# Down projection with the last 64 rows of its contraction as pairs of 64-row tiles, and a new order of all steps

## The chip, the cores and the metric

The kernel runs on one core of one Trainium2 chip. The metric is the device time of one execution in microseconds. The kernel before takes 234.98 us in the median of three runs (234.88 to 235.36). All inputs are bf16 in HBM, and so is the output.

## What is computed

Two independent branches read the same layer-normalised input and are added to it. Branch A is a gated long convolution (a four-tap shift convolution of k, times v, a convolution of length 2048 by FFT, times the normalised input). Branch B is a gated feed-forward layer.

```python
S, D, F = 2048, 640, 1728
xn = layernorm(A_q)
# branch A
k_shift = sum(k_pad[t:t + S] * shift_k[:, 3 - t] for t in range(4))
kv = k_shift * v
y = irfft(rfft(kv padded to 2 S) * rfft(ssm_k padded to 2 S))[:S] + kv * ssm_D
A = xn * y
# branch B
h = sigmoid(xn @ w_gate) * (xn @ w_up)        # 2048 x 1728
Bo = h @ w_down                               # 2048 x 640
out = A_q + A + Bo
```

## The kernel before

The 2048 tokens lie on 128 partitions with 16 blocks of 128 tokens each. x, the normalised xn, all weights and the output stay in SBUF; the result is added into x in place and stored from there.

**Branch B** goes in four stages t = 0 to 3 of 512 tokens (four blocks bb). In a stage, the 1728 hidden columns are 13 tiles of 128 and one of 64. For each of the 13, gate_mm and up_mm make two products of five matmuls of 128x512 each (product, L291), gate_ev takes the sigmoid on ACT (L300), up_ev multiplies on DVE and writes hT[:, fc, :] (L306). The last 64 gate columns and the last 64 up columns share one product (both_mm, L312): its upper 64 partitions hold the up half, and both_mul (L321) writes the 64 hidden rows to partitions 64 to 127 of hT[:, 13, :]. Partitions 0 to 63 of that tile are cleared once (L126), and so are those of wd[:, 13, :] (L127).

The down projection sums 14 tiles, fc = 0 to 13, for each token block. The first 512 output columns are down_mm (L329), 14 matmuls of 128x512 in two parts of seven, into one PSUM bank pd; down_ev (L334) adds the bank to x on DVE. The remaining 128 columns are rest_mm (L340), 14 matmuls of 128x128 for each block, and rest_ev (L345).

**Branch A** goes in five chunks c of 128 channels. Taps and products are on DVE (kv_op, L373 to L382), ssm_k is turned in place (h_turn, L359), and the transform has two stages of matmuls each way: st1_mm (L398, L400), through DRAM (wr1, rd2), st2_mm (L432, 32 matmuls of 32x32 tiles), a complex product on DVE (prod, L445 and L447), inv1_mm (L461, 32 matmuls of 32x32 tiles), through DRAM again (wr2, L477 and L481; rdb, L491), and inv2_mm (L500, eight matmuls of 128x128). inv2_q (L505) multiplies by xn, inv2_x (L510) adds to x. PSUM results of st1, st2 and inv1 are copied out by ACT (act_copy, L254) or by DVE (dve_copy, L257).

**PSUM.** Two pools share the eight banks: psC has two tiles of two banks (st1, st2, inv1), psG four tiles of one bank (gate, up, both, pd, pr, psb of inv2).

**The order** is written out by hand. Each kind of step fills a chain under a letter (from L565 on), and the string ORDER (L683) says which chain gives the next step: g is PE's work of branch B, s its ACT part, u its DVE part, a/b/c/d the matmuls of branch A, A/B/C their copies on ACT, I/F/J the same on DVE, p prod, q inv2_q and inv2_x, k kv_op, w/r/W/R the transfers through DRAM, m and n the loads, o the stores. TURNS (L694) permutes the loads and the stores. Each engine executes its own instructions in this order, and waits on semaphores for the others. Nearly all DMAs are issued from SP's queue; the last store goes through ACT's (L348).

In a stage the steps of the down projection come as (bb, part) = (0,0), (1,0), (0,1), (1,1), (2,0), (2,1), with down_ev after each second part, then (3,0), (3,1) and the rest. In stage 3 the rest of blocks 0 to 2 comes ahead of block 3.

Of the kernel before, what the change touches and what calls it, by code (L numbers as in the profile page):

```python
# [10 lines left out]
BF16 = mybir.dt.bfloat16  # L11
# [6 lines left out]
DM = 640  # L18
FF = 1728
P = 128  # L20
NB = S // P
NC = DM // P
NFC = 14
# [42 lines left out]
def kernel(  # L66
# [14 lines left out]
    nc = tc.nc  # L81
# [15 lines left out]
    res = ctx.enter_context(tc.tile_pool(name="res", bufs=1))  # L97
# [22 lines left out]
    w = res.tile([P, NC, 2 * FF], BF16, name="w")  # L120
    wd = res.tile([P, NFC, DM], BF16, name="wd")
    hT = res.tile([P, NFC, 512], BF16, name="hT")
    kxs = [res.tile([P, NB + 3, P], BF16, name="kx%d" % i) for i in range(2)]
    for kx in kxs:
        nc.gpsimd.memset(kx[0:1, 0:3, :], 0.0)
    nc.gpsimd.memset(hT[0:64, 13, :], 0.0)  # L126
    nc.gpsimd.memset(wd[0:64, 13, :], 0.0)  # L127
    nc.vector.memset(hT[:, 0, :], 0.0)
    warm = res.tile([P, 4], F32, name="warm")
    nc.scalar.activation(warm[:, :], mhalf[:, :], ACT.Sigmoid)  # L130
# [60 lines left out]
    def load_wd(eng, lo, hi):  # L191
        h = min(hi, 13)
        eng.dma_start(wd[:, lo:h, :], B_w_down[lo * P:h * P, :].rearrange("(c p) e -> p c e", p=P))
        if hi == NFC:
            eng.dma_start(wd[64:P, 13, :], B_w_down[13 * P:FF, :])


    lns = [dict() for _ in range(4)]
# [121 lines left out]
    def both_mul(t):  # L320
        nc.vector.tensor_tensor(hT[64:P, 13, :], sig[13][64:P, :], pgs[2, 13][64:P, :], ALU.mult)  # L321

    pds = {}

    def down_mm(t, bb, part):
        if part == 0:
            pds[bb] = psG.tile([P, 4 * P], F32, name="pd", tag="g")
        for fc in range(7 * part, 7 * part + 7):
            nc.tensor.matmul(pds[bb][:, :], lhsT=hT[:, fc, bb * P:(bb + 1) * P], rhs=wd[:, fc, 0:4 * P],  # L329
                             start=(fc == 0), stop=(fc == NFC - 1))  # L330

    def down_ev(t, bb):
        b = 4 * t + bb
# [233 lines left out]
    def step(k, fn, *args):  # L567
        chains[k].append((fn, args))

    for t in range(4):  # L570
        for fc in range(0 if t else 2, 13):
            step("g", gate_mm, t, fc)
            step("s", gate_ev, t, fc)
            step("g", up_mm, t, fc)
            step("u", up_ev, t, fc)
        step("g", both_mm, t)
        step("s", both_ev, t)
        step("u", both_mul, t)
        for bb, part in ((0, 0), (1, 0), (0, 1), (1, 1), (2, 0), (2, 1)):
            step("g", down_mm, t, bb, part)  # L580
            if part:
                step("u", down_ev, t, bb)
        last = [(0, 3), (3, 4)] if t == 3 else [(0, 4)]
        for b0, b1 in last:
            if b1 == 4:
                step("g", down_mm, t, 3, 0)
                step("g", down_mm, t, 3, 1)
                step("u", down_ev, t, 3)
            for bb in range(b0, b1):
                step("g", rest_mm, t, bb, b0)  # L590
            step("u", rest_ev, t, b0, b1)
# [10 lines left out]
    for k in ((load_w, sync, 512, 768, 0),  # L602
              (load_w, sync, 512, 768, 1),
              (load_taps, 0),
              (sync.dma_start, SMt[:], SMd.ap()),
              (load_w, sync, 768, 1024, 0),
              (load_w, sync, 768, 1024, 1),
              (load_w, sync, 1024, 1280, 0),
              (load_w, sync, 1024, 1280, 1),
              (load_wd, sync, 0, 7),  # L610
              *ks(0),
              (load_w, sync, 1280, FF, 0),
              (load_w, sync, 1280, FF, 1),
              *hs(0),
              *vs(0),
              (load_wd, sync, 7, NFC),
              (sync.dma_start, S1t[:], S1d.ap()),
              (sync.dma_start, FWt[:], FWd.ap()),
              *hs(1),
              (load_x, sync, 1),  # L620
              *ks(1),
              *vs(1)):
        step("m", *k)
# [54 lines left out]
    for b in (0, 4, 8, 12):  # L678
# [2 lines left out]
    step("o", store, NB - 1, NB, 4 * P, DM)  # L681

    ORDER = """  # L683
    mmmmmggsmgggsuuggsgmLgLumssZLLPmguggumggmsgmkmkkuslgsTkmkukuggsummgsmmHHmmggugDkksumlggsgllugkkkkkkk
    kHHaamAnggAtkaaImueeggkuuwAagaeeAAkkLggkgmuDgamwLgsAaAwkkkkmgLgsKKaAgakukkkkkgusuggAsTkugagtwaLkkgsI
    AuuggkkkakhHHgwnsauKKsgVAAPlgsauklTwIkLkkrgaggruwVAVsDlbgklBuggBsawuagAAgbgkkssgkkKkFuuatkBhaIgkgAwm
    paakLsprswkgupukKKKHAAwggLpaaAkugAgceuggCCbkkkHDkgkkLgBFkkeuuaapggAeAVpTgeurbFPBpgstgrbkuBggwBkaaskk
    gguIgAsgkksuKVhHrkwawAWaAkggDaAparApukgnkpkssgcCVJuuggbFwBWggssubBBkwppgskgaaIuuggrAcgpJgrpsuCbsFRWk
    BgsugupbBprgsBllgugscCdlrpdkukkkwegeqqClHbBBRggbBgWrFqaeIagAdaaquqqupdpgAAppwaaAuggrAqqucCeJRwgggbpw
    WBFpgugbrrdqpqgsdRgBBpcuggJqCWbgsusFBgsubggBppdBdpqqppcrsCCrguugsbFgguBsRbpggrrBpBdcqqqsWdqCggpCuqpq  # L690
    bFBRpruggsbWpBBuqsggcpJCdqusgupbdWBBggsqppgsugRcCJuqqggRdqqsWgdRugdqqqdquRogggqogguuqooooddqqqqogddo
    qqgggoqoquuuoooo
    """
    TURNS = {"m": [6, 0, 1, 4, 21, 5, 13, 2, 7, 15, 9, 10, 12, 14, 8, 17, 18, 11, 16, 20, 22, 23, 19, 25, 24, 26, 3],  # L694
        "o": [5, 0, 6, 3, 1, 7, 4, 2, 8, 10, 9, 11, 12, 13]}
    left = {k: iter([v[i] for i in TURNS.get(k, range(len(v)))]) for k, v in chains.items()}
    for k in "".join(ORDER.split()):
        fn, args = next(left[{"F": "B", "J": "C", "I": "A", "Y": "E"}.get(k, k)])
# [32 lines left out]
```

## Time and profile before

| | us |
|---|---|
| median of the runs | 234.98 |
| the profiled execution | 235.94 |
| its span, first to last instruction | 234.2 |
| PE busy (matmuls) | 227.0 |
| DVE busy | 204.1 |
| ACT busy | 131.5 |
| POOL busy | 12.7 |
| matmuls of gate and up, L291: 250 each | 62.2 each |
| matmuls of down, L329 (213 of 224 recorded) | 50.4 |
| matmuls of the rest, L340 | 13.8 |
| granted TensorE clock | 1.00 |

The span is the time from the first to the last instruction of one profiled execution; the execution's own time has a little more around it. A row of the timeline gives the start in us from the span's start, the busy time, the engine, the line, the operation, out<-in by tile names, the shape and the count. Matmuls overlap: the row of one says 379 ns for 128x512, though the next one starts earlier, so pitches are read from starts.

### The profile page before, as it was taken

The numbers are of one execution on the slowest core, as the hardware profiler recorded it, in microseconds if no ns is written. First come the engines' busy times: TensorE is split into PE (matmuls) and PEld (weight loads), VectorE is DVE, ScalarE is ACT, GpSimd is POOL, SyncE is SP. The second block draws the span as 40 slices with busy tenths as digits, with TensorE's granted clock in tenths as the row PEclk, the third lists the DMA queues.
The fourth block names the chain that finished last, engine by engine and source line by source line (L and its number), as shares of the span: only waits on it lengthen the run. The fifth ranks groups of instructions, "written<-read, shape, count | busy, mean of one in ns | idle before, by whom it ended". The sixth has DMA issues, their size and how long they took to land.

```text
span 234.2 us, 5584 instructions
## 1 busy us (share of the span) xinstructions
PE 227.0 (97%) x2270; PEld 112.8 (48%) x2281; DVE 204.1 (87%) x323; ACT 131.5 (56%) x191; POOL 12.7 (5%) x27
## 2 busy tenths in 40 slices
PE   7799999999999999999999999999999999999993
PEld 2664444447444444446444444445563545445582
DVE  5532789999969999999999999999999999999574
ACT  2347832438985877866647666855555776652000
POOL 5201200000020000012001000000000000000000
PEclk9999999999999999999999999999999999999999
DMA  6999999799789987978879998999989769784775
GB/s 176 278 305 235 246 344 203 208 243 304 198 270 293 317 213 211 249 164 243 212 261 266 309 272 214 271 227 258 321 200 247 213 180 255 182 217 145 216 266 148
DMA packets 98143, 56.07 MB, mean 239 GB/s; under 512 B 56326, under 2 KB 92358, under 8 KB 97990
## 3 DMA queue, kind: packets, MB, share of 16 engines
q1 hardware_dynamic: 97542, 55.35, 88.2%
q10 hardware_dynamic: 576, 0.36, 0.5%
q8 instruction: 18, 0.29, 0.5%
q14 instruction: 7, 0.06, 0.1%
HBM read 35.39 MB, written 18.35 MB: 229 GB/s over the span
## 4 chain that ended last, share of the span: by engine, by line
PE 79%; DVE 12%; DMA 4%; issue 2%; SPq 1%; ACT 1%; DVEq 0%
PE pg L291 22%; PE pu L291 22%; PE pd L329 14%; PE psb L500 3%; PE pr L340 3%; PE ps L400 3%; PE ps L398 3%; DMA w<-in_B_w_up_dram 3%; PE ps L432 3%; PE psa L461 2%; DVE tmp L377 2%; PE pg L312 1%; DVE acc L379 1%; DVE yx L505 1%; DMA SMt<-tabSM 1%
## 5 line engine op out<-in xcount | busy, mean ns | idle before, releaser
L291 PEld LDWEIGHTS <-w 128*128 128x128 bf16 x500 | 47.1, 98 | 57.4 <-issue 4.0
L291 PE MATMUL pu<-xnT,w 128*128 128x512 bf16 x250 | 62.2, 379 | 0.0
L291 PE MATMUL pg<-xnT,w 128*128 128x512 bf16 x250 | 62.2, 379 | 0.0
L329 PE MATMUL pd<-wd,hT 128*128 128x512 bf16 x213 | 50.4, 379 | 0.7 <-issue 0.2
L306 DVE TENSOR_TENSOR hT<-sig,pu 128x512 bf16<-128x512 bf16 x52 | 34.6, 679 | 12.8 <-ACT sig L300 6.9
L254 ACT CAST t<-ps 128x1024 bf16<-128x1024 f32 x33 | 32.3, 1013 | 21.9 <-PE ps L400 21.9
L300 ACT ACTIVATE sig<-pg 128x512 bf16<-128x512 f32 x52 | 30.6, 598 | 23.7 <-PE pg L291 20.1
L254 ACT CAST xz<-ps 128x1024 bf16<-128x1024 f32 x30 | 29.5, 1015 | 14.3 <-PE ps L432 14.3
L329 PEld LDWEIGHTS <-hT 128*128 128x128 bf16 x224 | 21.3, 98 | 25.1 <-issue 0.9
L447 DVE TENSOR_TENSOR xz<-xz 128x2048 bf16<-128x2048 bf16 x20 | 24.4, 1218 | 0.3
L377 DVE TENSOR_TENSOR tmp<-kx,sc 128x1024 bf16<-128x1024 bf16 x30 | 20.9, 698 | 0.4
L379 DVE TENSOR_TENSOR acc<-acc,tmp 128x1024 bf16<-128x1024 bf16 x30 | 20.6, 685 | 0.5
L505 DVE TENSOR_TENSOR yx<-psb,xn 128x512 bf16<-128x512 f32 x20 | 13.8, 688 | 2.6 <-PE psb L500 1.8
L400 PE MATMUL ps<-kvh,S1t 128*128 128x512 bf16 x40 | 15.5, 387 | 0.0
L254 ACT CAST ao<-psa 128x1024 bf16<-128x1024 f32 x11 | 10.8, 1014 | 8.3 <-PE psa L461 8.2
L398 PE MATMUL ps<-kvh,S1t 128*128 128x512 bf16 x40 | 15.1, 379 | 0.0
L445 DVE STREAM_SHUFFLE xz<-xz 128x512 f32<-128x512 f32 x20 | 14.5, 725 | 0.0
L340 PE MATMUL pr<-wd,hT 128*128 128x128 bf16 x224 | 13.8, 219 | 0.0
L340 PEld LDWEIGHTS <-hT 128*128 128x128 bf16 x224 | 13.0, 98 | 1.8 <-issue 0.6
L334 DVE TENSOR_TENSOR x<-pd,x 128x512 bf16<-128x512 f32 x16 | 10.7, 684 | 2.1 <-PE pd L329 2.0
L257 DVE CAST xz<-ps 128x1024 bf16<-128x1024 f32 x10 | 12.1, 1215 | 0.4 <-PE ps L432 0.4
L500 PEld LDWEIGHTS <-TBt 128*128 128x128 bf16 x160 | 9.7, 98 | 3.4 <-issue 1.5
(57 smaller groups left out, 183.9 us busy)
## 6 DMA issues: line engine op xcount, KB each, us to landing
d<-t SPq DMA_DIRECT2D x20, 512.0 KB, 5.1
t<-d SPq DMA_DIRECT2D x20, 512.0 KB, 5.5
bi<-d SPq DMA_DIRECT2D x8, 512.0 KB, 5.3
d<-ao SPq DMA_DIRECT2D x6, 512.0 KB, 5.7
kvh<-in_A_v_dram SPq DMA_DIRECT2D x10, 256.0 KB, 5.3
kx<-in_A_k_dram SPq DMA_DIRECT2D x10, 256.0 KB, 4.6
hn<-in_A_ssm_k_dram SPq DMA_DIRECT2D x20, 128.0 KB, 4.6
x<-in_A_q_dram SPq DMA_DIRECT2D x3, 640.0 KB, 5.1
```

The source lines that it names most:

```text
L254: nc.scalar.copy(out=out, in_=in_)
L291: nc.tensor.matmul(pg[:, :], lhsT=w[:, c, u * UP + fc * P:u * UP + (fc + 1) * P], rhs=xnT[:, :, c, :], start=(c == 0), stop=(c == NC - 1))
L300: nc.scalar.activation(sig[fc][:, :], pgs[0, fc][:, :], ACT.Sigmoid)
L306: nc.vector.tensor_tensor(hT[:, fc, :], sig[fc][:, :], pgs[1, fc][:, :], ALU.mult)
L329: nc.tensor.matmul(pds[bb][:, :], lhsT=hT[:, fc, bb * P:(bb + 1) * P], rhs=wd[:, fc, 0:4 * P], start=(fc == 0), stop=(fc == NFC - 1))
L340: nc.tensor.matmul(pds[t, b0][:, bb, :], lhsT=hT[:, fc, bb * P:(bb + 1) * P], rhs=wd[:, fc, 4 * P:DM], start=(fc == 0), stop=(fc == NFC - 1))
L377: nc.vector.tensor_tensor(d["tmp"][:, :, :], kx[:, lo + 3 - m:hi + 3 - m, :], sb(m), ALU.mult)
L379: nc.vector.tensor_tensor(d["acc"][:, :, :], d["acc"][:, :, :], d["tmp"][:, :, :], ALU.add)
L398: nc.tensor.matmul(ps[:, 0, :, :], lhsT=S1[:, h, :], rhs=cin[c]["kvh"][:, 0, 4 * n4:4 * n4 + 4, :], start=True, stop=True)
L400: nc.tensor.matmul(ps[:, 1, :, :], lhsT=S1[:, h, :], rhs=hp[:, 2 * n4:2 * n4 + 2, :, :], start=True, stop=True)
L447: nc.vector.tensor_tensor(z[:, 1:3, :, :], z[:, 0:1, :, :].to_broadcast((P, 2, 8, P)), z[:, 1:3, :, :], ALU.mult)
L500: nc.tensor.matmul(ps[:, i, :], lhsT=TB[:, h, 4 * m + i, :], rhs=bi[:, h, 4 * (m % 2) + i, :], start=(h == 0), stop=(h == 1))
```

## The change

A small tile hA of 64 partitions is added. After both_mul, a new step both_copy on ACT copies the 64 hidden rows of blocks 0 and 2 from partitions 64 to 127 of hT[:, 13, :] to partitions 0 to 63 of hA. down_mm leaves out fc 13: its second part has six matmuls in place of seven. A new step pair_mm adds what is left for all four blocks: blocks 0 and 2 from hA with a copy of the last 64 rows of w_down on partitions 0 to 63, blocks 1 and 3 from hT on partitions 64 to 127. Blocks 0 and 1 then have all their terms, and blocks 2 and 3 get their second part afterwards. So four accumulators are open at the same time. The 512 columns of w_down's last rows are loaded twice, and POOL clears only the 128 columns left for the rest, which is computed as before.

```diff
+    hA = res.tile([64, 2, P], BF16, name="hA")
...
-    nc.gpsimd.memset(wd[0:64, 13, :], 0.0)
+    nc.gpsimd.memset(wd[0:64, 13, 4 * P:DM], 0.0)
...
             eng.dma_start(wd[64:P, 13, :], B_w_down[13 * P:FF, :])
+            eng.dma_start(wd[0:64, 13, 0:4 * P], B_w_down[13 * P:FF, 0:4 * P])
...
+    def both_copy(t):
+        nc.scalar.copy(out=hA[:, :, :], in_=hT[64:P, 13, :].rearrange("p (b e t) -> p b e t", b=2, e=2)[:, :, 0, :])
...
-        for fc in range(7 * part, 7 * part + 7):
+        for fc in range(7 * part, 7 + 6 * part):
             nc.tensor.matmul(pds[bb][:, :], lhsT=hT[:, fc, bb * P:(bb + 1) * P], rhs=wd[:, fc, 0:4 * P],
-                             start=(fc == 0), stop=(fc == NFC - 1))
+                             start=(fc == 0), stop=(bb > 1 and fc == NFC - 2))
+
+    def pair_mm(t):
+        for bb in range(4):
+            lhsT = hT[64:P, 13, bb * P:(bb + 1) * P] if bb % 2 else hA[:, bb // 2, :]
+            rows = slice(64, P) if bb % 2 else slice(0, 64)
+            nc.tensor.matmul(pds[bb][:, :], lhsT=lhsT, rhs=wd[rows, 13, 0:4 * P], start=False, stop=(bb < 2))
...
         step("u", both_mul, t)
-        for bb, part in ((0, 0), (1, 0), (0, 1), (1, 1), (2, 0), (2, 1)):
+        step("s", both_copy, t)
+        for bb, part in ((0, 0), (1, 0), (0, 1), (1, 1), (2, 0), (3, 0)):
             step("g", down_mm, t, bb, part)
-            if part:
-                step("u", down_ev, t, bb)
+        step("g", pair_mm, t)
+        step("u", down_ev, t, 0)
+        step("u", down_ev, t, 1)
+        step("g", down_mm, t, 2, 1)
+        step("u", down_ev, t, 2)
         last = [(0, 3), (3, 4)] if t == 3 else [(0, 4)]
         for b0, b1 in last:
             if b1 == 4:
-                step("g", down_mm, t, 3, 0)
                 step("g", down_mm, t, 3, 1)
                 step("u", down_ev, t, 3)
```

ORDER is another string throughout: the same steps with the new ones among them, in another interleaving of the two branches, with three more st2 copies on ACT and three fewer on DVE, and one inv1 copy the other way. TURNS is new too: the loads of weights, k, v and the convolution kernel and the stores come in another sequence. In the last stage inv1_mm(9), the last of its kind, stands after the first part of block 0 of the down projection (before: ahead of both_mm), one store stands between wr2(9) and the reads rdb(4,0) and rdb(4,1), and the last steps are down_mm(3,3,1), inv2_mm(4,3), rest_mm of block 3, with down_ev, inv2_q, rest_ev and inv2_x behind them on DVE. The end of the string, before and after:

```diff
-    WBFpgugbrrdqpqgsdRgBBpcuggJqCWbgsusFBgsubggBppdBdpqqppcrsCCrguugsbFgguBsRbpggrrBpBdcqqqsWdqCggpCuqpq
-    bFBRpruggsbWpBBuqsggcpJCdqusgupbdWBBggsqppgsugRcCJuqqggRdqqsWgdRugdqqqdquRogggqogguuqooooddqqqqogddo
-    qqgggoqoquuuoooo
...
+    CggJswqbpBFupggsdqbBpguWqrrBpdqgscCJqugugbFBgppsuRgbBpggsuddqWqBrrscCJRgugbqqppBBWspggsrbrBBggupupdd
+    RqcJgsCpgsubFBprggsbBBuggpsqqudcCdgqJbquWpRRBBpggWgsgsppuugcCgJdqqqqgqddqgdqqWogqqsggguguRdRuqooodqqq
+    qoggudoogoqqodguoqouoqoo
```

More of the change, by code (lines that the diff above doesn't have):

```diff
@@ L683 @@
     ORDER = """
[L684 to L689, printed above, removed]
-    WBFpgugbrrdqpqgsdRgBBpcuggJqCWbgsusFBgsubggBppdBdpqqppcrsCCrguugsbFgguBsRbpggrrBpBdcqqqsWdqCggpCuqpq
-    bFBRpruggsbWpBBuqsggcpJCdqusgupbdWBBggsqppgsugRcCJuqqggRdqqsWgdRugdqqqdquRogggqogguuqooooddqqqqogddo
-    qqgggoqoquuuoooo
-    """
-    TURNS = {"m": [6, 0, 1, 4, 21, 5, 13, 2, 7, 15, 9, 10, 12, 14, 8, 17, 18, 11, 16, 20, 22, 23, 19, 25, 24, 26, 3],
-        "o": [5, 0, 6, 3, 1, 7, 4, 2, 8, 10, 9, 11, 12, 13]}
+    mmmmgggmssggmuLuLmsggsZgmugmgmLsuuggsmgggsmkLkgkkkumsmgkusmmgkPgmullmlgulHmgsusgmHmuggDgggmkksuskkaA
+    kkkanggkkHaTAAegKuHeawmtkegkkekLgugaAuAgkkaADLgguaawAukmgsgAkggTuLksakkkkkggsguuwLPAkmkaAsthgggsKaaH
+    HwVAAugukggaamwsskKKrukkkwkkAAklgggauADkksVggTbwlguBgakssglBkkkAuspprgbBgguBkasnkaKKwIggthTuaAkaugAI
+    suggawspHuLLklkVkkAkkawApggakaLsgkkAKkgeemgAceLPuuggrgHuuCCbBrekkwgVFgkgppDlkkaAauKAggwhsulbgtgBBrwk
+    suHaAaAggpsbBBpuWgsgkkwVgucggksrpprCCaaWIAsggukalusaIggukAbFggsuBpbBHsgggpugsswDFcunkpKkCRpkrgCrgsaw
+    aIguuAdqdbFqVBppggsWbrggBBqlcCpuJksggbqBuBkgpgrsbBggkkkkkuBaaIgeeuppRdqqepaewAdWArwaAgRaarugAIggqwuc
+    CggJswqbpBFupggsdqbBpguWqrrBpdqgscCJqugugbFBgppsuRgbBpggsuddqWqBrrscCJRgugbqqppBBWspggsrbrBBggupupdd
+    RqcJgsCpgsubFBprggsbBBuggpsqqudcCdgqJbquWpRRBBpggWsgsppuugcCgJdqqqqgqddqgdqqWogqqsggguguRdRuqooodqqq
+    qoggudoogoqqodguoqouoqoo
+    """
+    TURNS = {"m": [0, 1, 21, 7, 2, 23, 9, 4, 5, 15, 6, 10, 18, 12, 13, 14, 8, 22, 17, 11, 20, 16, 25, 24, 26, 19, 3],
+        "o": [3, 6, 1, 7, 4, 5, 2, 9, 10, 8, 0, 12, 11, 13]}
     left = {k: iter([v[i] for i in TURNS.get(k, range(len(v)))]) for k, v in chains.items()}
```

## The prediction

> **What bounds the kernel now.** I read the page's busy shares first, then the chain that ended last, then the timeline where the chain changes engine.
>
> ```profile
> PE 227.0 (97%) x2270; PEld 112.8 (48%) x2281; DVE 204.1 (87%) x323; ACT 131.5 (56%) x191; POOL 12.7 (5%) x27
> ...
> PE 79%; DVE 12%; DMA 4%; issue 2%; SPq 1%; ACT 1%; DVEq 0%
> ```
>
> PE is busy 97% of 234.2 us and carries 79% of the chain. DVE, at 87%, is the chain's other engine. Whether a busy PE is a full PE is read from the starts in the timeline:
>
> ```profile
> 203.35 1.24 PE L291 MATMUL pu<-xnT,w 128*128 128x512 bf16 x5
> ...
> 204.52 0.44 PE L432 MATMUL ps<-t,FWt 32*32 32x256 bf16 x32
> ...
> 204.89 0.62 PE L500 MATMUL psb<-bi,TBt 128*128 128x128 bf16 x8
> ...
> 205.35 1.24 PE L291 MATMUL pg<-xnT,w 128*128 128x512 bf16 x5
> ...
> 206.43 1.24 PE L291 MATMUL pu<-xnT,w 128*128 128x512 bf16 x5
> ...
> 208.59 1.24 PE L291 MATMUL pu<-xnT,w 128*128 128x512 bf16 x5
> ...
> 209.76 0.65 PE L461 MATMUL psa<-xz,SMt 32*32 32x512 bf16 x32
> ...
> 210.34 1.25 PE L312 MATMUL pg<-xnT,w 128*128 128x512 bf16 x5
> ```
>
> 205.35 to 206.43 is 1.08 us for five matmuls: 0.216 each. L500 does eight of 128 columns in 0.46 us: 0.056 each. The groups follow at this pitch almost everywhere, so PE's own work is the span. Between 14 and 229 us I find only four waits that this pitch does not explain, 0.86 us together: 0.22 at 93.3, 0.23 at 102.4, 0.31 at 114.4, 0.10 at 117.1. The third is seen in one row: a block of L432 takes 0.82 here and 0.44 above.
>
> ```profile
> 114.43 0.82 PE L432 MATMUL ps<-t,FWt 32*32 32x256 bf16 x32
> ```
>
> So PE work removed is time won, as long as no wait takes its place.
>
> **The pairs.** Each of the four stages loses four matmuls of 128x512 (fc 13 of L329): 4 x 0.216 = 0.864 us. It gains four of 64 rows in two pairs. No row shows 64-row tiles; the nearest are the blocks of 32x32 tiles. From 208.59, five matmuls end their turn at 209.67, and L461 starts at 209.76: 0.09 to change into small tiles. The block then takes 0.58 for 32 matmuls of 512 columns on 16 tiles, two turns, 2 x 0.216 = 0.432 if a turn is fully side by side: 0.15 more, which is the way back and the stagger of 32 starts. L432 gives the same: 203.35 + 1.08 = 204.43, start 0.09 later, 0.37 for 2 x 0.108, 0.15 more. So a change there and back costs up to 0.24 with 32 tiles. Two pairs cost 0.43 plus something near that: at best 0.43 (changes free, -0.43 a stage), at worst 0.864 + 0.24 = 1.10 (one after the other, +0.24 a stage). I take 0.65, nearest the L461 block with fewer starts: 0.21 won a stage, **-0.86 us** in four.
>
> The Trainium skill (TensorEngine Tiling (Array Packing), Key Properties) says that changing the tiling mode drains the array. A matmul's row is 379 ns long and its pitch 216, so emptying would be 0.163 each way and a pair step 0.432 + 0.326 = 0.76, -0.42 us in four. The 0.09 before L461 and L432 is shorter than that, so the rows side with the smaller price on the way in.
>
> **What goes with it.** ACT gets four copies of 64x256 (nearest row: 0.65 for 128x512 of L162), and the new letters move two evacuations from DVE to ACT: 3 B more and 3 F fewer, 1 C fewer and 1 J more, so 2 x 1.22 us less on DVE, 2 x 1.02 more on ACT. ACT is 56% busy. The copy waits for both_mul, and pair_mm for the copy. Behind the copy on ACT stand the evacuations that free PE's psC banks, so a late both_mul would hold PE twice. From both_mul's turn to pair_mm PE has 20 matmuls of L329 or more, over 4.3 us, against 0.69 for both_mul and at most 0.65 for the copy; the copy's own turn comes after at least 12 of them. DVE would have to be some 3 us late, and the latest I find it is 2.4 (L334 at 109.84, its matmuls done at 107.4). Past that PE waits one for one. POOL clears 64x128 of wd, not 64x640 (0.62 us at 2.4 us, nobody waits). SP issues one more DMA, 64 KB of wd, about 0.5 us in its queue. Before it stand 9.3 MB where 9.0 MB stood, 0.3 MB at 240 GB/s or 1.3 us, so fc 7 to 12 land near 38.0 (before: issued 28.08, 8.67 to land, 36.75). They are used after 14 matmuls of L329, past 41.8: covered. Weight tiles of the first stage land at least 3 us ahead by the same count of bytes: gate tile 6 is there after 4.1 MB, about 18 us, and is used at 22.4.
>
> **The new order.** PE has the same 30 blocks of 32x32 tiles, so no changes of tile are saved, save one pair next to inv1_mm. The old order's 0.86 us of waits go with it, and others come. I lined up each engine's new order with these pitches. Two waits stand out. The built program lets inv1_mm(7) wait for the first half of prod(16). From inv1_mm(6) on, DVE must do a copy 1.13, three up_ev 1.8, inv2_q and x 1.07, prods 0.75 + 1.14 + 0.62 + 1.14 + 0.75: 8.4, after 0.76 for the block and its evacuation's start, 0.3 of leftovers: 9.4. PE has 0.58 + 6 x 1.08 + 2 x 0.46 + 0.9 = 8.9. PE waits 0.5. In the last stage all four accumulators are open at once, so down_mm(3,2,0) needs a bank that psb held, and DVE frees it by inv2_q: 0.3. With as much again for what I don't see, 1.0 comes for 0.86: **+0.1**. Above nothing it reaches 2 (the t=1 stage, where the chain runs on DVE from 89 to 114); below, all 0.86 gone.
>
> **The end.** It is read in these rows:
>
> ```profile
> 229.52 0.94 PE L340 MATMUL pr<-wd,hT 128*128 128x128 bf16 x14
> 229.92 0.68 DVE L334 TENSOR_TENSOR x<-pd,x 128x512 bf16<-128x512 f32 x1
> 230.52 0.28 DVE L345 TENSOR_TENSOR x<-pr,x 128x128 bf16<-128x128 f32 x1
> 230.83 0.35 ACTq L348 DMA_DIRECT2D out_dram<-x  x1
> ```
>
> PE ends at 230.46, the last addition at 230.80, 0.34 later; then a store of 2.33 to land. In the new order inv2_mm(4,3) stands between the last down matmul and the last rest, so DVE does down_ev 0.60, inv2_q 0.60, rest_ev 0.30, inv2_x 0.43 after that down matmul, 1.93, while PE has 0.45 + 0.78 = 1.23 left: it ends 0.7 to 0.8 after PE, **+0.4**, and +0.1 for arriving late from inv2_x(4,2). The last SP store (96 KB, 2.58 to land at 230.05) now waits for that addition, against 2.33: +0.15, with SP issuing 12 stores at about 0.55 each from inv2_x(3,3) on, just enough.
>
> **Sum:** -0.86 + 0.1 + 0.5 + 0.15 = **-0.1 us**. The profiled execution has a span of 234.2 within 235.94; I expect 234.1 in its terms. The runs shown have a median of 234.98, so 234.9.
>
> **Rivals.** *The new waits stay away* and the tail is as short as now: -0.86 - 0.5 + 0.5, or -0.86 + 0.1: about **234.2**. For it: DVE has 2.4 us less to do. Against: 1.9 us of DVE work counted after the last down matmul. *The last block's round trip comes late* (slower): inv1_mm(9) now stands after down_mm(3,0,0), inside the down stage. From it to inv2_mm(4,0) PE has 0.67 + 39 x 0.216 + 32 x 0.056 + 0.65 + 0.79 = 12.3 us. The trip took 2.09 to the write's issue, 3.83 to land, 0.06, and 5.77 for a read like that of 205.55: 11.75. Margin 0.55, where the old order had 2.3 (223.85 against 221.5); and a store that waits for inv2_x(3,1) now stands on SP between write and read. Reads of 6.93 (t<-d, 121.47) and 7.52 (72.08) are in the trace; at those PE waits 0.6 to 1.2 us with nothing behind it, in the tail. From a trip over 12.3 us it decides: **236.0**. *The pairs run one after the other*: +0.96 in place of -0.86, **236.7**. Against: L461 starts 32 matmuls in 0.58 us, and each pair writes two banks. *Full emptying at each change*: +0.44, **235.3**, the rule cited above.
>
> **Chances.** Forecast (234.4 to 235.4) 0.42; waits stay away 0.24; late trip 0.20; one after the other 0.06; emptying 0.08. Under 0.2%, 0.47 us, a measurement of this kernel can't tell from no change: faster is below 234.5, slower above 235.45. Faster: 0.22 of the second case and 0.05 of the forecast's edge, 0.27. Slower: 0.20 + 0.06 and 0.06 of edges, 0.32. Within: 0.41. The range 234.0 to 236.2 takes in the second and third case and leaves out the worst pairs.
>
> **What would show it.** pair_mm: four 64-row matmuls with two starts under 60 ns apart, 0.65 us from the previous group's turn to the next group's start; 1.1 would mean no overlap. A gap on PE before inv1_mm(7), near 196 us, of 0.3 to 0.7, ended by DVE. PE's last matmul about 0.7 us earlier, at 229.7, and DVE 0.7 to 0.9 us behind it. No gap before inv2_mm(4,0); a gap there is the third case. Wrong altogether: a PE gap over 0.5 us elsewhere, above all in 89 to 114 us, or loads late before 30 us.

## The result and the profile after

The changed kernel takes 237.06 us in the median (236.90 to 238.36, six runs) against 234.93 for the kernel before on the same chip: 2.13 us slower. The recorded ratio is 1.0106 with a 95% interval of [1.0091, 1.0121]; that of the two medians alone is 1.0091. The prediction was 234.9 with a range of 234.0 to 236.2.

The profiled execution of the changed kernel took 238.36 us, span 236.5. Both profiled executions happen to lie above their medians, by 1.0 us before and 1.3 after: before's PE waited 1.3 us for the first gate weights (its first 128x512 product starts at 13.75 us, and at 12.4 to 13.6 in all the others), and in after's a wait at 47 us was longer than in the runs that follow. So sizes below come from medians, or from differences within one trace.

From the page of the changed kernel, engines first, then the chain that ended last:

```profile
PE 227.2 (96%) x2281; PEld 112.0 (47%) x2281; DVE 202.1 (85%) x321; ACT 134.7 (57%) x197; POOL 12.1 (5%) x27
...
PE 63%; DVE 15%; SPq 9%; DMA 8%; issue 3%; DVEq 0%
```

The engines look the same. The chain doesn't: PE carried 79% of it and now 63%; SP's queue went from 1% to 9%, DMA from 4% to 8%. SP's queue and the transfers now hold parts of the chain that PE held. The timeline of the changed kernel over its last 20 us shows the pairs, and the first of two places where a transfer is waited for, the stores at the end:

```profile
218.22 0.38 SPq L359 DMA_DIRECT2D out_dram<-x  x1
...
219.04 3.18 PE L334 MATMUL pd<-wd,hT 128*128 128x512 bf16 x14 [0.16 <-DVE yx L516]
...
222.15 0.39 PE L341 MATMUL pd<-wd,hA 64*128 64x512 bf16 x1
222.16 0.39 PE L341 MATMUL pd<-wd,hT 64*128 64x512 bf16 x1
...
222.38 0.38 PE L341 MATMUL pd<-wd,hA 64*128 64x512 bf16 x1
222.38 0.38 PE L341 MATMUL pd<-wd,hT 64*128 64x512 bf16 x1
...
222.69 1.47 PE L334 MATMUL pd<-wd,hT 128*128 128x512 bf16 x6
...
224.92 0.42 DVE L521 TENSOR_TENSOR x<-x,yx 128x512 bf16<-128x512 bf16 x1
225.37 7.83 SPq L359 DMA_DIRECT2D out_dram<-x  x12
...
229.42 0.94 PE L351 MATMUL pr<-wd,hT 128*128 128x128 bf16 x14
229.90 0.68 DVE L516 TENSOR_TENSOR yx<-psb,xn 128x512 bf16<-128x512 f32 x1
230.50 0.28 DVE L356 TENSOR_TENSOR x<-pr,x 128x128 bf16<-128x128 f32 x1
230.81 0.43 DVE L521 TENSOR_TENSOR x<-x,yx 128x512 bf16<-128x512 bf16 x1
231.27 0.35 ACTq L359 DMA_DIRECT2D out_dram<-x  x1
```

The pairs do what they should. 14 matmuls from 219.04 end their turn at 222.06; the first two 64-row tiles start together at 222.15, the next two 0.22 later, and L334 at 222.69. The step takes 0.63 us where the four full matmuls took 0.86.

The end is different. DVE adds its last result at 231.24, but the span ends at 236.5. One store is issued at 218.22; after two reads, SP stands until inv2_x(3,3) (224.92) is done and then issues twelve stores in 7.83 us. After the last matmul (230.37) 6.12 us pass, against 3.70 before. In the kernel before, SP issues stores from 218.69 on, and inv2_x(3,3) comes at 223.21:

```profile
218.69 12.39 SPq L348 DMA_DIRECT2D out_dram<-x  x13
...
223.21 0.42 DVE L510 TENSOR_TENSOR x<-x,yx 128x512 bf16<-128x512 bf16 x1
```

SP's waits at the stores, first of the kernel before (total, times, longest):

```profile
SPq L348 <- DVE x L510: 4.8, 3, 4.0
```

and of the changed kernel:

```profile
SPq L359 <- DVE x L521: 9.1, 2, 5.4
```

What the longer stand means is read from the DMA share in two-microsecond windows of the changed kernel (busy time of the engines, clock, DMA share, GB/s):

```profile
222.00:224.00 2.00, 2.00 (x13) 0.72 (x12) 1.29 (x2) 0.00 (x0) 0.00 (x0) 1.00 0.94 348
224.00:226.00 2.00, 2.00 (x37) 2.00 (x36) 1.67 (x3) 0.00 (x0) 0.00 (x0) 1.00 0.06 20
...
230.00:232.00 2.00, 0.37 (x7) 0.19 (x4) 1.20 (x3) 0.00 (x0) 0.00 (x0) 1.00 0.73 211
232.00:234.00 2.00, 0.00 (x0) 0.00 (x0) 0.00 (x0) 0.00 (x0) 0.00 (x0) 1.00 0.98 288
```

From 224 to 226 the DMA engines do almost nothing (20 GB/s) while finished rows of x wait behind one that isn't finished; from 232 to 234, with every engine done, they run at 0.98. In the kernel before these two windows have 0.73 and 0.09:

```profile
224.00:226.00 2.00, 2.00 (x40) 2.00 (x38) 1.37 (x3) 0.00 (x0) 0.00 (x0) 1.00 0.73 245
...
232.00:234.00 2.00, 0.00 (x0) 0.00 (x0) 0.00 (x0) 0.00 (x0) 0.00 (x0) 1.00 0.09 24
```

The second place is early. The changed kernel's timeline of 30 to 50 us has

```profile
32.91 0.59 SPq L167 DMA_DIRECT2D kx<-in_A_k_dram  x1
...
40.68 2.75 PE L334 MATMUL pd<-wd,hT 128*128 128x512 bf16 x12 [0.18 <-DMA wd<-in_B_w_down_dram]
...
41.99 0.69 DVE L384 TENSOR_TENSOR acc<-kx,sc 128x1024 bf16<-128x1024 bf16 x1 [4.20 <-DMA kx<-in_A_k_dram]
...
48.55 0.39 PE L409 MATMUL ps<-kvh,S1t 128*128 128x512 bf16 x1 [1.22 <-DVE kvh L393]
```

PE waits a little for weights (0.35 against its pitch). DVE waits 4.20 us for the second half of k of chunk 0, whose load SP issued at 32.91, behind both parts of wd (2.2 MB), with the first half of k of chunk 1 far ahead of it. In the kernel before this load stands behind wd too, but is issued at 29.84: in the changed kernel SP stands 2.8 us in front of a small load (the last rows of k of chunk 1, issued at 29.63) that now lies between the two parts of wd. Some five us after DVE's wait, PE waits for what DVE makes of the half of k (1.22 in the row, 1.38 against PE's pitch).

So there are three theories for the +2.1: (1) the stores' new turn, (2) the loads' new turn, (3) the pairs themselves or the order around them.

### The profile page after: what moved, and what is told of

It is laid out like the page before. It is cut to its first block, busy times and chain, and to the rows that moved or that the text cites. A ratio compares the mean times of both kernels' runs of the same rounds, so it can differ in the third digit from the quotient of the medians.

```text
span 236.5 us, 5598 instructions
## 1 busy us (share of the span) xinstructions
PE 227.2 (96%) x2281; PEld 112.0 (47%) x2281; DVE 202.1 (85%) x321; ACT 134.7 (57%) x197; POOL 12.1 (5%) x27
## 4 chain that ended last, share of the span: by engine, by line
PE 63%; DVE 15%; SPq 9%; DMA 8%; issue 3%; DVEq 0%
PE pg L293 16%; PE pu L293 16%; PE pd L334 13%; PE pr L351 4%; DMA kx<-in_A_k_dram 4%; PE ps L409 4%; PE ps L411 4%; DMA w<-in_B_w_up_dram 3%; DVE yx L516 3%; PE ps L443 2%; PE psa L472 2%; SPq L185 2%; DVE x L521 2%; SPq L188 2%; DVE xz L458 2%
## 5 line engine op out<-in xcount | busy, mean ns | idle before, releaser
L334 PE MATMUL pd<-wd,hT 128*128 128x512 bf16 x208 | 48.4, 379 | 0.3 <-DMA wd<-in_B_w_down_dram 0.2
L256 ACT CAST xz<-ps 128x1024 bf16<-128x1024 f32 x33 | 32.4, 1017 | 16.8 <-PE ps L443 16.8
L334 PEld LDWEIGHTS <-hT 128*128 128x128 bf16 x208 | 19.7, 98 | 24.9 <-issue 2.7
L351 PEld LDWEIGHTS <-hT 128*128 128x128 bf16 x224 | 13.1, 98 | 2.0 <-issue 0.6
L370 DVE STREAM_TRANSPOSE kvh<-hn 128x512 f32<-128x512 f32 x10 | 10.9, 1096 | 0.0
```

Source lines behind the costliest of these rows:

```text
L256: nc.scalar.copy(out=out, in_=in_)
L351: nc.tensor.matmul(pds[t, b0][:, bb, :], lhsT=hT[:, fc, bb * P:(bb + 1) * P], rhs=wd[:, fc, 4 * P:DM], start=(fc == 0), stop=(fc == NFC - 1))
```

## The experiments

Each kernel was timed together with the kernel before on the same chip; the times are medians in us, and a ratio is against the kernel before. All compute the whole output.

**The stores alone.** e1_stores puts those that are ready first:

```diff
-        "o": [3, 6, 1, 7, 4, 5, 2, 9, 10, 8, 0, 12, 11, 13]}
+        "o": [3, 1, 2, 0, 4, 5, 6, 7, 8, 9, 10, 12, 11, 13]}
```

> The changed kernel with one list altered: the sequence in which SP issues the stores. The five stores that need nothing but chunks 0 to 3 go ahead of the one that waits for inv2_x(3,3) and down_ev. Theory 1, late stores: in the changed kernel SP stands from 219.97 to 225.37 us at that one store, the DMAs are idle from 224 to 226 (share 0.06), and 12 stores then take until 235.35. Then this takes off what the last store lands after the last addition (235.35 - 231.24 = 4.1 us) less the 2.36 of the kernel before: -1.5 to -2 us, 235.1 to 235.5. Theory 2, waits in the middle (loads late, 40 to 49 us): no change, 237.0. Theory 3, the pairs cost more than they save: no change, 237.0.

Measured 235.53 (ratio 1.0029 [1.0014, 1.0044]): 1.53 us of the 2.13 come back. From its last matmul to its end 4.06 us pass, and the DMA share is 1.08 from 224 to 226.

**The pairs alone.** e2_nopair takes them out, with the copy to hA and the second load, and leaves the new order:

```diff
-            lhsT = hT[64:P, 13, bb * P:(bb + 1) * P] if bb % 2 else hA[:, bb // 2, :]
-            rows = slice(64, P) if bb % 2 else slice(0, 64)
-            nc.tensor.matmul(pds[bb][:, :], lhsT=lhsT, rhs=wd[rows, 13, 0:4 * P], start=False, stop=(bb < 2))
+            nc.tensor.matmul(pds[bb][:, :], lhsT=hT[:, 13, bb * P:(bb + 1) * P], rhs=wd[:, 13, 0:4 * P],
+                             start=False, stop=(bb < 2))
```

> The changed kernel without the pairs: in the same place and order the four blocks' fc 13 are four matmuls of 128x512 over all 128 rows, with no copy, no second load of the last rows, and the old clearing. Theory 1 and 2: a pair step takes 0.63 us from the previous group's turn to the next group's start, four matmuls 0.86, so PE ends 4 x 0.24 = 0.95 us later; the end is held by stores that start at a DVE step behind PE, so 0.6 to 1.0 us slower than the changed kernel, 237.6 to 238.1. Theory 3, the pairs cost more than they save: faster than the changed kernel, 236.5 or less.

Measured 237.86 (1.0131 [1.0117, 1.0144]), 0.80 slower than with pairs. The pairs gain; theory 3 in its first form falls.

**The loads alone.** e3_loads puts the second half of k of chunk 0 between the two parts of wd, where it stood behind both. The first half of k of chunk 1, which stood sixth of all loads, and the small load between the parts of wd go behind them:

```diff
-    TURNS = {"m": [0, 1, 21, 7, 2, 23, 9, 4, 5, 15, 6, 10, 18, 12, 13, 14, 8, 22, 17, 11, 20, 16, 25, 24, 26, 19, 3],
+    TURNS = {"m": [0, 1, 21, 7, 2, 9, 4, 5, 15, 6, 10, 18, 12, 13, 14, 8, 11, 17, 22, 23, 20, 16, 25, 24, 26, 19, 3],
```

> The changed kernel with one list altered: the sequence of the loads. The second half of k of chunk 0 goes ahead of the second part of w_down, and the first half of k of chunk 1, which nobody needs yet, goes behind it. Theory 2: DVE stands 4.2 us until 41.99 for that half of k, and st1_mm then stands 1.38 us at 47 for DVE; both go, and the end comes 1 to 1.4 us sooner, 235.7 to 236.1. Theory 1: PE gains the same 1 to 1.4 us at 47, but it is passed on only as far as the steps that release the stores come sooner too, so between 0.5 and 1.4. If neither: 237.0.

Measured 236.93 (1.0083 [1.0070, 1.0096]), 0.13 faster than the changed kernel by the medians and some 0.5 by the ratios. Both waits are gone in its profile, and its last matmul ends at 228.82, 1.54 us sooner than in the changed kernel's. The end still comes 6.1 us after that matmul, so it is 1.56 sooner too. The late stores don't hide a faster PE: their start moves with PE (225.37 there, 223.84 here), and e2_nopair lost 0.80 with the same late stores.

The medians differ less than the profiles because the wait itself comes and goes. At 47 us PE lost 1.38 in the changed kernel's profile; e1_stores is the same program up to its stores and lost 0.71 there, and in the profile of e2_nopair, whose loads differ only by the 64 KB of the second copy, no such wait is seen. Four of the changed kernel's six executions took 236.90 to 237.10, like e3_loads, and the other two about 1 us more.

**Both.** e4_both has the two edits together.

> Both lists altered, stores and loads. Theory 1 and 2 together: the gains add, -2.5 to -3.4 us, 233.7 to 234.5, below the kernel before (234.93) by the pairs' 0.95 less the longer tail. Theory 3: no better than 236.5.

Measured 234.82 (1.0000 [0.9992, 1.0009]). With the stores cured, the loads are worth 0.71 by the medians, but the eight executions of e1_stores reach from 234.90 to 236.69, and six and four executions stand behind the 0.13 above; that the two numbers differ is not shown to be more than chance. With the loads cured, the stores are worth 2.11, and the traces agree: from DVE's last addition to the end 5.25 us pass in the changed kernel and 5.23 in e3_loads, 3.20 in e1_stores and 3.21 here.

**The stores' turn in the old kernel.** e5_before_late leaves before's matmuls and arithmetic as they are and lets SP stand at a store that isn't ready; the end of ORDER and the stores' list:

```diff
-    gdqqqdquRogggqogguuqooooddqqqqogddoqqgggoqoquuuoooo
+    gdqqqdquRogggqgguuqddqqoooooqqogddoqqgggoqoquuuoooo
...
-        "o": [5, 0, 6, 3, 1, 7, 4, 2, 8, 10, 9, 11, 12, 13]}
+        "o": [5, 8, 6, 0, 3, 1, 7, 4, 2, 10, 9, 11, 12, 13]}
```

> The kernel before, with its matmuls and its arithmetic untouched; only its last stores are put in another turn, so that one of them goes out early, as in the changed kernel, and SP then stands at a store that needs inv2_x(4,0) (done at 225.65 in the profile of before; in the changed kernel SP was let go at 225.37), with eleven others behind it that were ready before. Theory (the changed kernel's loss is SP's queue: what stands behind a store that isn't ready): twelve issues of 0.6 from 225.65 on end at about 232.8 in place of 230.6, so 2.0 to 2.4 us slower than before, 236.9 to 237.3. Rival (the loss is in the new order of PE's and DVE's last steps, and the queue has room): the kernel before stays within 0.3 us, 234.9 to 235.2.

Measured 237.55 (1.0110 [1.0097, 1.0124]): 2.6 us lost with not one matmul moved, a little more than the 2.0 to 2.4 expected. (Of the stores behind the one that isn't ready, seven were ready, where the expectation says eleven; the other four need later steps.) Its windows have the same two marks, an empty one and a full one after the engines are done:

```profile
224.00:226.00 2.00, 1.95 (x32) 1.72 (x30) 1.77 (x4) 0.00 (x0) 0.00 (x0) 1.00 0.16 37
...
232.00:234.00 2.00, 0.00 (x0) 0.00 (x0) 0.00 (x0) 0.00 (x0) 0.00 (x0) 0.59 0.89 243
```

**The pairs with both cures.** e6_nopair_both is e4_both with the pairs taken out as in e2_nopair.

> The changed kernel with both cures (stores that are ready go first; the half load of k ahead of the late weights), and without the pairs: the last 64 rows as four full products of 128 rows per stage, whose upper half of rows holds zeros, as before. Theory (a pair step takes 0.63 us where a full one takes 0.86): 4 times 0.237, 0.8 to 0.95 us slower than the kernel with both cures, 235.6 to 235.8. Rival (the stores set the end whatever PE does): within 0.3 us of it, 234.8 to 235.1.

Measured 235.66 (1.0032 [1.0019, 1.0044]), 0.84 slower than e4_both. The pairs are worth the same 0.8 with and without the late stores. Without them the new order, both queues cured, is 0.69 slower than before; so e4_both, equal to before, still loses about that somewhere in its order.

**The end.** e7_end is e4_both with inv2_mm(4,3) moved ahead of the last down group:

```diff
-    qqgqddqgdqqWogqqsggguguRdRuqooodqqqqoggudoogoqqodguoqouoqoo
+    qqgqddqgdqqWogqqsggguguRdRuqooodqqqqogguddoogoqqqqoguoouooo
```

> The changed kernel with both cures, and inv2_mm(4,3) moved ahead of the last down group, its two DVE steps ahead of down_ev(3,3). Theory (the prediction's term for the end, 0.5: DVE ends 0.87 us after the last matmul because three steps of inv2 and rest_ev stand behind it): DVE ends 0.3 to 0.4 after the last matmul, which itself stays, so 0.5 us faster than with both cures, 234.3. Rival (SP's last stores set the end, not the last DVE step): 0.2 us or less, 234.6 to 234.8.

Measured 235.18 (1.0006 [0.9994, 1.0018]), 0.36 above e4_both: no gain, a miss. Its timeline says why:

```profile
228.21 0.69 DVE L516 TENSOR_TENSOR yx<-psb,xn 128x512 bf16<-128x512 f32 x1
228.93 0.42 DVE L521 TENSOR_TENSOR x<-x,yx 128x512 bf16<-128x512 bf16 x1
229.28 0.68 DVE L345 TENSOR_TENSOR x<-pd,x 128x512 bf16<-128x512 f32 x1
229.88 0.28 DVE L356 TENSOR_TENSOR x<-pr,x 128x128 bf16<-128x128 f32 x1
```

DVE goes through the same steps in another order without a pause over 0.15 us from 224 us on, and ends 1.07 us after PE. The end looks like DVE's throughput and not its order. The other reading was that SP's last stores set it. Against that stands the time from DVE's last addition to the end, 3.21 us in e4_both, 3.26 here and 3.24 in e13_yx2 below: the end moves with DVE.

**A wait.** e8_end_prod is e7_end and also moves the first half of prod(16) ahead of up_ev(3,7):

```diff
-    ...rbrBBggupupdd
+    ...rbrBBgguppudd
```

> As the run before, and the first half of prod(16) moved one step ahead on DVE, before up_ev(3,7), so that inv1_mm(7) finds it done. Theory (PE's wait of 0.38 in front of inv1_mm(7), at 194 us, is for this shuffle alone, which ended at 194.4): about 0.3 us faster than the run before, 234.0. Rival (what is late next takes its place: up_ev(3,7) is 0.7 us later and holds a bank): no difference, 234.3.

Measured 234.88 (0.9997 [0.9988, 1.0006]), 0.30 below e7_end, as expected; PE's wait there is gone. Against e4_both (234.82) the two moves together bring nothing.

**The pairs in the old order.** e9_pairs_old has before's order with pairs in stages 0 to 2 only.

```diff
+        if t < 3:
+            step("s", both_copy, t)
+            for bb, part in ((0, 0), (1, 0), (0, 1), (1, 1), (2, 0), (3, 0)):
+                step("g", down_mm, t, bb, part)
+            step("g", pair_mm, t)
```

> The order, the loads and the stores of the kernel before, with the pairs in stages 0 to 2 and the full product kept in stage 3; in these three stages alone the steps move that the pairs force (block 3's first half ahead of them, the adds of blocks 0 and 1 behind them, one inv2_mm behind them so that four banks suffice). Theory (a pair step saves 0.24 a stage, and what the changed kernel lost was lost by its new order): 3 times 0.237, about 0.7 us faster than before, 234.2. Rival (four banks held until the pairs cost their own waits in any order, on PE or on DVE, which then has three adds in a row): 0.4 or more a stage, 234.9 or above.

Measured 241.76 (1.0301 [1.0276, 1.0325]), 6.8 slower: a miss by far. Its waits (DVE's, then PE's) name two queues:

```profile
DVE x L345 <- PE pd L341: 4.9, 1, 4.9
...
PE ps L409 <- DVE xz L259: 3.0, 1, 3.0
```

The adds of blocks 0 and 1, put right behind the pairs, made DVE wait 4.9 us with its other work behind them. e11_pairs_old2 sets them, and the copies of hA, later:

> As e9_pairs_old, with what stood wrong in its queues set right: in stage 1 the adds of blocks 0 and 1 stand behind five more DVE steps (DVE waited 4.87 us for the pair there and PE then 3.0 us for DVE), and hA's copy stands behind the evictions that it held up on ACT in stages 1 and 2 (PE then waited 1.4 and 1.27 us for ACT). Theory (the 6.8 us of that run were these two places in line, the pairs themselves save 0.237 a stage): the waits of 3.0, 0.9 and 1.27 go and the time falls to 234.2 to 235.0. Rival (four banks held until the pair cost several us in the old order wherever the adds stand): above 237.

Measured 235.26 (1.0016 [1.0005, 1.0027]): 6.5 of the 6.8 came from where the steps stood. It still misses its upper expectation, 235.0, by 0.26. From the first 128x512 product to the last matmul PE takes 217.3 us, against 216.7 in before's profile; waits of 0.57, 0.37 and 0.39 at 113, 156 and 164 us (before: one of 0.38, in the same measure, at 114) eat the 0.7 of three pair steps and more.

**DVE's load at the end.** e10_pool is e8_end_prod with two of DVE's adds on POOL:

```diff
-        nc.vector.tensor_tensor(xs, xs, chunks[c]["yx", m][:, :, :], ALU.add)
+        eng = nc.gpsimd if c == 4 and m < 2 else nc.vector
+        eng.tensor_tensor(xs, xs, chunks[c]["yx", m][:, :, :], ALU.add)
```

> The kernel with both cures and both moved steps, with two of DVE's last adds (inv2_x(4,0) and inv2_x(4,1)) on POOL, which does nothing then. Theory (the last 7 us are DVE's: it runs without a gap from 223 us to its end, so that reordering its steps gains nothing and only fewer steps do): two times 0.53 go from DVE, which is then held by the last matmul, 0.3 to 0.6 us faster than the run without POOL, 234.3 to 234.6. Rival (the last stores set the end, through SP's queue): no difference, 234.9; POOL and DVE could also slow each other, then slower.

Measured 236.15 (1.0050 [1.0038, 1.0062]), slower by 1.3 than e8_end_prod: yx has one buffer, and DVE's next multiply waits until POOL has read it.

```profile
226.96 1.15 POOL L522 TENSOR_TENSOR x<-x,yx 128x512 bf16<-128x512 bf16 x1 [0.80 <-DVE yx L516]
...
228.14 0.69 DVE L516 TENSOR_TENSOR yx<-psb,xn 128x512 bf16<-128x512 f32 x1 [0.80 <-POOL x L522]
```

e12_pool2 gives yx a second buffer; e13_yx2 has that buffer and no POOL; e14_before_yx2 puts it into the kernel before:

```diff
-        chunks[c]["yx", m] = yx = cv.tile([P, 4, P], BF16, name="yx")
+        chunks[c]["yx", m] = yx = cv.tile([P, 4, P], BF16, name="yx", bufs=2)
```

> As e10_pool, with a second buffer for yx, for whose one buffer DVE waited behind POOL there (1.27 and 0.80 us, POOL's add taking 1.15 where DVE's takes 0.42). Theory (DVE's run of steps sets the end): two adds of 0.53 less on DVE, 234.3 to 234.6, against 234.88 with neither. Rival (the last stores set the end through SP): 234.9; or POOL's add slows DVE's next to it: DVE's multiplies longer than 0.69 and the time above 234.9.

> As e8_end_prod, with the second buffer for yx alone, nothing on POOL. e12_pool2 was 1.1 us faster than e8_end_prod by two edits: two of DVE's adds on POOL, and two buffers for yx, with which an inv2_q starts 0.35 us after the inv2_x ahead of it where it started 0.53 after it. Theory (the buffer: its 0.18 a step ends the waits of 0.5 and 0.33 for a bank at 214 and 217 us in the profile of e8_end_prod): 0.7 of the 1.1, 234.1 to 234.2. Rival (POOL's relief of DVE at the end is the whole gain): 234.9.

> The kernel before with a second buffer for yx and nothing else. Theory (the waits for a bank in stage 3 are the new order's own, which holds four banks until the pairs; the old order shows none at these places): 0 to 0.3 us faster than before, 234.6 to 234.9. Rival (the buffer helps either order as much, since DVE's last 8 us hold the end of both): 0.7 faster, 234.2.

Measured: e12_pool2 233.78 (0.9954 [0.9939, 0.9969]), e13_yx2 233.80 (0.9954 [0.9942, 0.9967]), e14_before_yx2 234.81 (0.9994 [0.9985, 1.0003]). The buffer is the whole gain, 1.08 us on the new order (more than the 0.7 expected), and 0.15 or nothing on the old one. POOL adds nothing. In stage 3, where four banks are open, the timeline of e8_end_prod has

```profile
214.11 0.69 DVE L516 TENSOR_TENSOR yx<-psb,xn 128x512 bf16<-128x512 f32 x1
214.84 0.42 DVE L521 TENSOR_TENSOR x<-x,yx 128x512 bf16<-128x512 bf16 x1
214.85 0.61 PE L511 MATMUL psb<-kx,TBt 128*128 128x128 bf16 x8 [0.34 <-DVE yx L516]
...
215.37 0.69 DVE L516 TENSOR_TENSOR yx<-psb,xn 128x512 bf16<-128x512 f32 x1
```

and that of e13_yx2

```profile
213.79 0.68 DVE L516 TENSOR_TENSOR yx<-psb,xn 128x512 bf16<-128x512 f32 x1
...
214.51 0.43 DVE L521 TENSOR_TENSOR x<-x,yx 128x512 bf16<-128x512 bf16 x1
214.53 0.61 PE L511 MATMUL psb<-kx,TBt 128*128 128x128 bf16 x8
214.85 0.69 DVE L516 TENSOR_TENSOR yx<-psb,xn 128x512 bf16<-128x512 f32 x1
```

From the start of an add to the start of the next multiply 0.53 us pass with one buffer and 0.34 with two. DVE frees the banks earlier: PE's waits at 214.85 and 217.37, 0.51 and 0.33 against its pitch, shrink to 0.12 in all, and the last DVE step ends 0.65 us after the last matmul (1.07 in e8_end_prod). e13_yx2, the changed kernel with its stores, its loads, two steps and one buffer set right, is 1.16 us faster than the kernel before, 0.46% with an interval of 0.33 to 0.58.

## Why the prediction was wrong

Sign and range were wrong; the terms of its sum, one by one:

- **The pairs, 0.65 us a step, -0.86: right.** 0.63 in the trace, 0.80 and 0.84 by e2_nopair and e6_nopair_both. The rival "one after the other" falls: the two tiles of a pair start at the same time. So does full emptying, which asked for 0.76 a step: the trace has 0.09 into the small tiles and 0.09 out beyond the pitch (0.31 from the second pair's start to the next group, at a pitch of 0.22). The Trainium skill (TensorEngine Tiling (Array Packing), Key Properties) says that a change of mode drains the array, and that different tiles can run in parallel. The second is what the trace shows; of the first, 0.09 each way is all that is seen, not the 0.163 that the prediction derived for that rival.
- **The last SP store, +0.15: the step that failed.** It read "with SP issuing 12 stores at about 0.55 each from inv2_x(3,3) on, just enough". Twelve stores it was, but they start later and take longer. inv2_x(3,3) now ends 5.03 us ahead of PE's end (225.34 of 230.37), where it ended 6.83 ahead of it (223.63 of 230.46). In both kernels it stands behind the adds of blocks 0 to 2 on DVE, but the first half of block 3 (7 x 0.216 = 1.51 us) now comes ahead of the second half of block 2 on PE. The prediction gives no time for inv2_x(3,3); "just enough" fits only the old one, 223.63 + 12 x 0.55 = 230.2. And twelve issues took 7.83 us and not 6.6: eleven at 0.57, and one of 1.57. So the last issue is at 232.74 and lands 2.61 later, 4.11 us after DVE's last addition, where the last store landed 2.36 after it before. e1_stores prices this at 1.53 and the two kernels with cured loads at 2.11, and e5_before_late shows the same loss on the old kernel. The queue's order was read, and its start not placed anew.
- **Loads, "covered": wrong.** The prediction counted bytes ahead of wd and of the gate weights, and named a late load before 30 us as what would prove it wrong. It put the landing of the second part of wd near 38.0 and its use past 41.8; the use came at 40.68, and PE waited for the landing there (0.35 against its pitch). It left out the half load of k behind wd, which DVE needs at 38 us, and SP's stand of 2.8 us ahead of it. PE pays another 1.38 in the profile; in the medians the loads cost 0.13 or 0.71, for the wait comes and goes.
- **New waits, 1.0 for 0.86: the new ones right in place and size, the old ones not.** In e4_both, PE loses 0.38 in front of inv1_mm(7) (0.09 of it is the change into small tiles) and 0.36 and 0.32 for banks, 1.06 in all. But two of the four old waits, 0.22 at 93.3 and 0.23 at 102.4, are none: PEld has one weight load of L329 more there than PE has matmuls, so the record of a matmul is missing, as for 11 of L329's 224. The term was thus nearer +0.4 than +0.1: from the first 128x512 product to the last matmul PE takes 216.71 us before and 217.11 in e6_nopair_both. No gap came before inv2_mm(4,0): the late round trip, the slower rival with 0.20, did not happen. The slow side came from a mechanism that had no place among the rivals.
- **The end, +0.5: right in size, half right in cause.** DVE ends 0.87 us after PE (0.34 before). The prediction blamed the place of inv2_mm(4,3); in e7_end another place brings nothing, and in e13_yx2 a shorter turn of DVE does.

The sum in medians: pairs -0.84, stores +1.53, loads +0.71; what remains of the +2.13 is 0.73 for the new order's waits and DVE's end, near the +0.6 forecast for them. (Curing the loads first gives +0.13 for them and +2.11 for the stores, with the same sum.) With both queues cured the kernel takes 234.82, against the 234.9 forecast, and part of that is luck: in the traces the waits are 0.3 worse than forecast, the pairs 0.1 better, and the time from DVE's last addition to the end is 0.15 shorter than before, where 0.15 more was forecast.

What stays open: why the waits of the old order, once pairs are put into it (e11_pairs_old2), eat the 0.7 that they should bring. Only their places were seen, and no run takes them away one at a time.

## What to carry to other kernels

When a change reorders a queue, place again the event that its head waits for, and count what stands behind it; a DMA window near zero in the last stage, followed by a full one after the engines are done, is that fault. A wait for a transfer can come and go from one execution to the next (the loads: 0.13 between one pair of kernels, 0.71 between another), so before saying that one limit hides another, take more executions and compare traces from the same matmul on. And a single buffer between two steps of one busy engine is worth a look as soon as more accumulators are held open: one more cost nothing here and gave 1.08 us.

## What the runs showed of the hardware

Two 64-row tiles of one pair start within 0.01 us of each other (222.15 and 222.16) and the next pair 0.22 us later, with two banks written at once. A POOL add of 128x512 bf16 takes 1.15 us where DVE's takes 0.42, and two of them beside DVE's multiplies (0.69 alone, 0.68 to 0.69 there, in e12_pool2) didn't slow these. Writing a buffer that the same engine has just read costs DVE 0.19 us a step against another buffer (0.53 and 0.34 from start to start). Of the twelve late stores in the changed kernel's profile, one held SP for 1.6 us (229.41 to 231.03), where the others took 0.4 to 0.8. The same store takes 1.57 us in the profiles of e2_nopair and e3_loads; what holds it is not shown.
